# Attention scores on four 64x64 quarters of the array, in tiles of 64 queries by 192 keys

## The chip, the cores and the metric

The program runs on one core of one Trainium2 chip. The metric is the device time of one execution in microseconds (us). Names of engines: PE is the matrix engine (TensorE), PEld its weight loads, DVE the vector engine, ACT the scalar engine, POOL GpSimd, SP the engine that issues the DMAs. PSUM is the memory that PE writes, in banks.

## The reference, cut to what matters

Windowed attention (a query sees itself and the 127 keys before it, with a bias that falls linearly with distance, steeper for some heads), then a gated MLP whose gate mixes positions, then a token-shift block.

```python
def _attn_ref(q, k, v):                      # (4, 8, 576, 64) each
    scores = scale * q @ k.T
    rel = pos[:, None] - pos[None, :]
    slopes = 2.0 ** (-8.0 * (np.arange(H) + 1) / H)
    bias = slopes[:, None, None] * (-np.abs(rel))
    mask = (rel >= 0) & (rel < 128)
    scores = np.where(mask, scores + bias, -1e9)
    attn = exp(scores - max); attn = attn / (sum(attn) + 1e-09)
    return attn @ v
...
def _moe_ref(x, w_in, g_ln, w_sg, b_sg, w_out):   # x (4, 576, 512), d_ff 1024
    h = gelu(x @ w_in); u, v = h[..., :512], h[..., 512:]
    v_n = layernorm(v) * g_ln
    v_s = einsum('ts,bsd->btd', w_sg, v_n) + b_sg[None, :, None]
    return x + (u * v_s) @ w_out
...
def _moe2_ref(x, mu_k, mu_r, w_k, w_v, w_r):
    xk, xr = token-shift mixes of x
    return sigmoid(xr @ w_r) * (relu(xk @ w_k) ** 2 @ w_v)
```

## The kernel before

The 32 heads are taken in 16 pairs; a pair's q and k lie transposed in SBUF, one head on partitions 0 to 63 and the other on 64 to 127 (`rawqk`, 64 is the head's width). The MLP and the last block work in fp32r, the attention in full fp32: PE runs an fp32 matmul as two records in the trace, each streaming its columns twice.

**Scores.** `s_items` takes 128 queries by 256 keys (128 for the first tile): the two heads of a pair run side by side on the two halves of the array's rows, each into a PSUM bank of its own. The last 64 queries are one matmul of 64 by 192 for each head on two 64x64 quarters, into one bank (`last_items`). `s_tile` follows each score tile: DVE adds the mask and takes the row's extreme (`nmax`), ACT takes the exponential with the row sum, and, for heads from 8 on (`fold`), DVE or POOL adds the two key halves onto each other, so that 256 keys become 128 columns with two triangles to be told apart later.

**Probabilities times v.** The probabilities are turned by PE transposes (`t1_step`, `t2_step`, `t4_step`): 7 of them for each of the first 8 heads, 4 for a folded one, and 1 for a pair's last queries. For folded heads `keep` splits the triangles, on POOL by affine_select or on DVE by a multiplication with `tri`. `av_items` multiplies v (128 keys by 64) by up to 256 columns; the heads of a pair use the two halves of the array's columns.

**Where it stands.** `slot(c)` is the work of a pair. From pair 5 on two groups stand on PE: `av_s` (the pair before times v, then the first half of this pair's scores) and `s_rest` (the last 64 queries, then the second half). `moe1(b)` is the MLP of batch b; `merge` mixes the next pairs' attention into it. `phase2` is the last block. The mask comes from the DMA `rel`, the identity for transposes from the DMA `ident`; DVE and POOL turn `rel` into 8 masks and 4 for the last queries (`mask_head`).

**What sets the order.** A list scheduler in the kernel (`Rec.schedule`) orders the instructions of all engines by latest start plus the numbers in `PRI`, and picks the engine where there are several (`ENG`). Each engine then runs its queue strictly in that order. Where PE would stand empty early on, the scheduler puts filler matmuls (`wps<-tri`) that compute nothing.

Of the kernel before, what the change touches and what calls it, by code (L numbers as in the profile page):

```python
# [20 lines left out]
P = 128  # L21
# [27 lines left out]
    ("vsg", "dve/pool"): -122084, ("vsg.1", "dve"): 2660, ("vsg.1", "dve/pool"): -32242, ("w_in_t.0", "act/dve/pool"): -34846,
    ("w_in_t.0", "dve/pool"): 16462, ("w_out_t.1", "act/dve/pool"): 9, ("w_out_t.1", "dve/pool"): -16447, ("w_r_t", "act/dve/pool"): -4065,  # L50
    ("w_r_t", "dve/pool"): -22022, ("w_sg_t.1", "dve/pool"): -208885, ("w_v_t", "act/dve/pool"): -3901, ("w_v_t", "dve/pool"): -2737,
    ("wdec", "act"): 24174, ("wdec", "dve"): 74457, ("wdec.0", "dve"): 34851, ("wdec.1", "act"): 46, ("wdec.1", "dve"): 112585,
# [1284 lines left out]
```

## Time and profile before

| | us |
|---|---|
| device time, median of 3 runs (592.68 to 592.96) | 592.87 |
| span of the profiled execution, first to last instruction | 591.1 |
| PE busy | 578.8 (98%) |
| DVE, ACT, POOL busy | 422.5, 301.9, 158.4 |
| start to the first matmul with `w_sg` (0 to 92.81): PE, DVE busy | 85.96, 81.50 |
| 92.81 to 278.00 (attention inside the MLP): PE busy | 185.19 |
| 278.00 to 586.64 (rest of the MLP, last block): PE busy | 307.65 |

The profiled execution's own device time is not listed; its span stands 1.8 us under the median, which is what lies around the span. A busy PE includes fillers and weight loads that are not hidden, so a group's cost is read from the starts of the matmuls ahead of it and behind it, not from its busy time.

### The profile page before, as it was taken

The page shows a single profiled execution, that of the slowest core. Times are in us where ns is not written, and L with a number is a line of the kernel's source. Part 1 is how long each engine was busy: PE and PEld are TensorE (multiplying, and loading weights), DVE is VectorE, ACT ScalarE, POOL GpSimd, SP SyncE. Part 2 cuts the span into 40 slices and gives each one's busy share as a digit, 9 for nine tenths or more (in the row PEclk, how much of TensorE's full clock was granted, in tenths as well). Part 3 has the DMA queues.
Part 4 walks back from the last instruction along what each step waited for, and adds up shares of the span by engine and source line. Part 5 has one row for each costly group of instructions (what it writes and reads, how often), then busy time and mean ns, then how long its engine had stood idle before and what let it go on. Part 6 is the DMA issues. An engine that isn't in the chain of part 4 may idle for free.

```text
span 591.1 us, 10011 instructions
## 1 busy us (share of the span) xinstructions
PE 578.8 (98%) x3579; PEld 482.2 (82%) x3579; DVE 422.5 (71%) x1149; ACT 301.9 (51%) x790; POOL 158.4 (27%) x287
## 2 busy tenths in 40 slices
PE   7999999999999999999999999999999999999996
PEld 4666688987899878989799987888888888888895
DVE  5998999986979769887799999972945162615221
ACT  4977876646666546733564387440413441442141
...
DMA packets 23282, 48.29 MB, mean 82 GB/s; under 512 B 4416, under 2 KB 13120, under 8 KB 22720
## 3 DMA queue, kind: packets, MB, share of 16 engines
...
q14 instruction: 22, 0.18, 0.1%
...
## 4 chain that ended last, share of the span: by engine, by line
PE 87%; DMA 5%; DVE 4%; ACT 2%; issue 0%; POOL 0%; SPq 0%; ACTq 0%; DVEq 0%
PE d L466 51%; PE vps L466 17%; PE rps L466 8%; PE s L466 5%; PE a L466 4%; DMA st<-in_w_in_dram 3%; PE tf L474 2%; DMA rawv<-in_v_dram 1%; DMA rawqk<-in_qk_dram 1%; DVE p L810 1%; PE t L474 1%; ACT p L571 1%; DMA wraw<-in_w_sgT_dram 0%; DVE w_sg_t L508 0%; DVE wdec L561 0%
## 5 line engine op out<-in xcount | busy, mean ns | idle before, releaser
L466 PE MATMUL d<-xk,wk 128*128 128x512 f32 (+1 forms) x480 | 102.1, 368 | 0.0
L466 PEld LDWEIGHTS d<-xk,wk 128*128 128x128 f32 x480 | 84.0, 188 | 15.6
L466 PE MATMUL vps<-w_v_t,k2h 128*128 128x512 f32 x288 | 95.5, 395 | 0.0
L488 ACT ACTIVATE p<-p,nmax 128x256 f32<-128x256 f32 (+1 forms) x144 | 67.5, 471 | 29.1 <-DVE nmax L810 28.2
L466 PEld LDWEIGHTS vps<-w_v_t,k2h 128*128 128x128 f32 x288 | 54.1, 188 | 12.9
L466 PE MATMUL d<-w_sg_t,vhl 128*128 128x288 f32 x448 | 63.8, 298 | 0.0
L508 DVE TENSOR_TENSOR k2l<-rl,k2h 128x512 fp32r<-128x512 f32 (+1 forms) x40 | 24.9, 635 | 53.6 <-ACT k2h L496 53.1
L466 PEld LDWEIGHTS d<-w_sg_t,vhl 128*128 128x128 f32 x448 | 60.3, 188 | 2.0 <-issue 2.0
L466 PE MATMUL d<-w_in_t,xg 128*128 128x512 f32 (+1 forms) x240 | 60.9, 401 | 0.9 <-ACT xg L496 0.6
L466 PE MATMUL vps<-w_v_t,k2l 128*128 128x512 f32 x144 | 57.0, 396 | 0.0
L810 DVE CUSTOM_DVE_ANT_0 p<-s,mask 128x256 f32<-128x256 f32 (+1 forms) x144 | 48.1, 381 | 11.0 <-PE s L466 10.7
L466 PE MATMUL d<-gg,w_out_t 128*128 128x288 f32 x384 | 55.2, 297 | 0.0
L466 PE MATMUL rps<-w_r_t,xr 128*128 128x512 f32 x216 | 53.7, 392 | 1.0 <-ACT r L488 1.0
L466 PE MATMUL d<-xg,w_in_t 128*128 128x288 f32 x384 | 54.3, 298 | 0.2 <-DVE u L544 0.2
L466 PEld LDWEIGHTS d<-xg,w_in_t 128*128 128x128 f32 x384 | 51.6, 188 | 2.7 <-issue 1.0
L466 PEld LDWEIGHTS d<-gg,w_out_t 128*128 128x128 f32 x384 | 52.0, 188 | 1.8 <-issue 1.3
L466 PEld LDWEIGHTS d<-w_in_t,xg 128*128 128x128 f32 (+1 forms) x240 | 41.2, 177 | 15.0 <-issue 2.0
L466 PEld LDWEIGHTS rps<-w_r_t,xr 128*128 128x128 f32 x216 | 40.4, 188 | 10.4 <-ACT r L488 1.4
L508 DVE TENSOR_TENSOR r<-vps,r 128x512 f32<-128x512 f32 x18 | 12.4, 690 | 47.8 <-ACT r L488 32.9
L466 PE MATMUL s<-rawqk 64*128 64x256 f32 (+2 forms) x320 | 42.2, 371 | 1.8 <-DMA rawqk<-in_qk_dram 0.9
L488 ACT ACTIVATE rl<-d 128x512 f32<-128x512 f32 (+1 forms) x40 | 22.0, 554 | 41.9 <-PE d L466 36.4
L527 POOL TENSOR_SCALAR_AFFINE_SELECT pf<-pf 128x512 f32<-128x512 f32 (+2 forms) x58 | 34.0, 598 | 23.2 <-ACT pf L496 11.8
(120 smaller groups left out, 946.5 us busy)
## 6 DMA issues: line engine op xcount, KB each, us to landing
...
```

The costliest lines, as they stand in the source:

```text
L466: pe.matmul(real(o), real(l), real(r), start=st, stop=sp, **ex)
L474: pe.transpose(real(o), real(i), real(d))
L488: nc.scalar.activation(real(out), real(in_), func, scale=scale, **kw)
L508: alts.append(("dve", self._dve(out.n, False), lambda: nc.vector.tensor_tensor(real(out), real(a), real(b), op)))
L527: nc.gpsimd.affine_select(out=real(out), in_=real(in_), pattern=[[0, rows], [sgn, n]], compare_op=cmp, fill=0.0, base=0, channel_multiplie ...
L571: alts.append(("act", self._act(a, 1), lambda: nc.scalar.mul(real(out), real(a), real(s1))))
L810: K.raw("dve", 70 + w / 0.96, lambda: nc.vector.tensor_tensor_reduce(out=real(pw), in0=real(s), in1=real(ma), scale=-0.125, scalar=3.0e38, ...
```

## The change

Scores are taken in tiles of 64 queries, n = 0 to 8, by the 192 keys that they can see (64 and 128 for the first two). Query block n of head j goes to output partitions 64p with p = j for even n and the other half for odd n, so that four matmuls, two heads by two blocks, use the four 64x64 quarters; an even block and the odd one after it lie in two banks. The two heads of a pair share one tile of 128 partitions, with 9 tiles for a pair as before. Every tile with 192 keys is folded to 128 columns (7 for a pair, in all pairs), so all pairs need 9 transposes. In the products with v a matmul has 128 columns, not up to 256, and there are 14 where there were 8 (beside the 4 of 64 columns). `rel` and `ident` are made on POOL (iota, affine_select, memset), the DMAs for them go, and there are 4 masks of 2 by 192. `PRI` and `ENG` are new numbers throughout.

```diff
 PRI = {
...
-    rel = T("up", [P, MW], F32, "u", "rel")
+    rel = T("up", [P, 192], F32, "u", "rel")
-    K.tri = T("attc", [P, 2, 4, P], BF16, "tri")
+    K.tri = T("attc", [P, 2, 8, 64], BF16, "tri")
...
+    def s_item(c, n, bank, k):
+        w, k0 = width(n), 64 * max(n - 2, 0)
+        raw, it = rawqk[c], []
+        for p in range(2):
+            j = p ^ (n % 2)
+            r = slice(64 * j, 64 * j + 64)
+            it.append((bank[64 * p:64 * p + 64, k, 0:w], raw[r, 0, 64 * n:64 * n + 64], raw[r, 1, k0:k0 + w], True, True, SG))
+        return it
+    def s_items(c, half):
         banks = [T("psS", [P, 2, 256], F32, "s") for _ in range(2)]
-        for k, i in enumerate(ii):
-            q0 = i * P
-            k0, w = (q0 - P, 256) if i else (0, P)
-            for j in range(2):
-                r = slice(64 * j, 64 * j + 64)
-                it.append((banks[j][:, k, :w], rawqk[c][r, 0, q0:q0 + P], rawqk[c][r, 1, k0:k0 + w], True, True, {}))
+        return banks, [x for k in range(2) for o in range(2) for x in s_item(c, 4 * half + 2 * k + o, banks[o], k)]
...
-        if i == 4 or i and fold(n):
-            K.tt(p[:, :w - P], p[:, :w - P], p[:, P:w], ALU.add, "dp")
+        f = 64 if n % 2 and n > 1 else 0
+        if n > 1:
+            K.tt(p[:, 2 * f:2 * f + 64], p[:, 0:64], p[:, 128:192], ALU.add, "dp")
+        elif n == 0:
+            z = p[:, 64:128]
+            K.raw("pool", 110, lambda: nc.gpsimd.memset(real(z), 0.0), [], [z])
+        PT[c, n] = p[:, f:f + 128]
...
+    def t_step(c, b):
+        K.transposes([(t[:, 2 * i:2 * i + 2, :].flat(), PT.pop((c, 4 * b + i)), ident) for i in range(4)])
+        K.copy(pf[:, i0:i0 + 8, :].flat(), t.flat())
+        m = 4 if b == 0 else 0
+        K.keep(pf[:, 14 + i0 + m:22 + i0, :], pf[:, i0 + m:i0 + 8, :], True, "dp")
+        K.keep(pf[:, i0:i0 + 8, :], pf[:, i0:i0 + 8, :], False, "dp")
...
+        for t in range(4):
+            for j in range(2):
+                its.append((a[64 * j:64 * j + 64, 2 * t:2 * t + 2, :], rv[j][:, t, :], pair(4 * t, j), t == 0, t == 3, SG))
+            if t < 3:
+                for j in range(2):
+                    its.append((a[64 * j:64 * j + 64, 2 * t + 2:2 * t + 4, :], rv[j][:, t, :], pair(18 + 4 * t, j), False, False, SG))
...
-    K.dma(rel, relc, P * MW * 4)
-    K.dma(ident, identc, P * P * 4)
+    def rel_rows(v):
+        K.raw("pool", 290, lambda: nc.gpsimd.iota(...), [], [v])
+        K.raw("pool", 285, lambda: sel([[-1, 192]], 128, 1, ALU.is_ge), [v], [v])
+        K.raw("pool", 285, lambda: sel([[1, 192]], 0, -1, ALU.is_gt), [v], [v])
+    for j in range(2):
+        rel_rows(rel[64 * j:64 * j + 64])
...
+    def mask_pair(c):
+        K.ts(mask[:, c], mask[:, 0], 4.0 ** -c, 0.0, ALU.mult, ALU.add, "dp")
```

On PE, one pair inside the MLP. Names: `a` is the product with v, `s` a score bank, `tf` a transpose, `d` the MLP. Before, a pair inside a product with `w_out_t`:

```order
L466 MATMUL a<-pf,rawv 64x256 x6
L466 MATMUL a<-pf,rawv 64x128 x2
L466 MATMUL a_2882<-pf_2831,rawv 64x64 x4
L466 MATMUL s<-rawqk 128x128 x2
L466 MATMUL s<-rawqk 128x256 x2
L466 MATMUL d<-gg,w_out_t 128x288 x12
L466 MATMUL s<-rawqk 64x192 x2
L466 MATMUL s<-rawqk 128x256 x4
L466 MATMUL d<-gg,w_out_t 128x288 x42
```

and after, a pair inside a product with `w_out_t`:

```order
L472 MATMUL a<-pf,rawv 64x128 x14
L472 MATMUL a_1950<-pf,rawv 64x64 x4
L472 MATMUL s<-rawqk 64x64 x2
L472 MATMUL s<-rawqk 64x128 x2
L472 MATMUL s<-rawqk 64x192 x4
L472 MATMUL d<-gg,w_out_t 128x288 x18
L472 MATMUL s<-rawqk 64x192 x10
L472 MATMUL d<-gg,w_out_t 128x288 x42
```

The second score group had two forms, a 64x64 and a 64x128 one, and now has one form.

POOL at the start, before (`tri` is the triangle mask, `w_in_t` the split of the first weights):

```order
L1187 MEMSET tri 128x1024
L881 MEMSET x 128x4 x2
L527 ISA
L527 AFFINE_SELECT tri<-tri 128x512 x2
L564 TENSOR_SCALAR mask_147<-rel 64x192 x6
L564 TENSOR_SCALAR mask<-rel 128x320 x3
L510 TENSOR_TENSOR w_in_t<-wdec,w_in_t 128x512
```

and after:

```order
L1196 MEMSET ident 128x128
L820 MEMSET p 128x64 x2
L1197 ISA
L1197 AFFINE_SELECT ident<-ident 128x128
L820 MEMSET p 128x64
L1186 IOTA rel 64x192 x2
L1185 AFFINE_SELECT rel<-rel 64x192 x4
L877 MEMSET x 128x4
L1199 MEMSET tri 128x1024
L877 MEMSET x 128x4
L534 AFFINE_SELECT tri<-tri 128x512 x2
L516 TENSOR_TENSOR p<-p 128x64 x3
```

`tri` comes behind `rel` and `ident`; PE's filler ahead of the first score matmul reads `tri`. The eight subtractions that write `w_in_t`, all on POOL before, are on DVE after.

DVE's queue up to the first layernorm statistic of batch 0 (`bn`) changes by these counts. New: 8 subtractions `w_in_t` of 128x512, 20 folds `p` of 128x64, 6 triangle products `pf` of 128x128 and 2 of 128x256, 3 casts `xg` of 128x576, 2 products `p` with `rin`. Gone: 3 copies `pf` of 128x384 and 3 of 128x512 (one more of 128x512 comes from `tf`), 1 copy `rt`, 4 folds of 128x128, 1 cast `w_in_t`, 1 step `gt`. The score steps were 30 of 256 columns, 10 of 128 and 5 of 192, and are 35 of 192, 5 of 128 and 5 of 64; the masks were 5 of 320 and 2 of 64x192, and are 3 of 384 and 4 of 64x192.

PE at the program's end, before (`vps` and `rps` are the two products of the last block; `r` needs the sigmoid of `rps` and then `vps`):

```order
L466 MATMUL vps<-w_v_t,k2h 128x512 x2
L466 MATMUL vps<-w_v_t,k2l 128x512
L466 MATMUL vps<-w_v_t,k2h 128x512
L466 MATMUL rps<-w_r_t,xr 128x512 x12
L1333 UNCONDITIONAL_BRANCH
```

and after:

```order
L472 MATMUL rps<-w_r_t,xr 128x512 x12
L472 MATMUL vps<-w_v_t,k2h 128x512
L472 MATMUL vps<-w_v_t,k2l 128x512
L472 MATMUL vps<-w_v_t,k2h 128x512 x2
L472 MATMUL vps<-w_v_t,k2l 128x512
L472 MATMUL vps<-w_v_t,k2h 128x512 x2
L472 MATMUL vps<-w_v_t,k2l 128x512
L472 MATMUL vps<-w_v_t,k2h 128x512 x2
L472 MATMUL vps<-w_v_t,k2l 128x512
L472 MATMUL vps<-w_v_t,k2h 128x512
```

The last matmuls are now those of `vps`, not those of `rps`.

## Rows read from the trace of the kernel before

**Rows 1.** Stage; its length; busy PE, PEld, DVE, ACT, POOL; clock; DMA share, GB/s

```profile
0.00:92.81 92.81, 85.96 (x655) 61.91 (x656) 81.50 (x269) 70.01 (x221) 54.28 (x101) 1.00 0.61 171
92.81:278.00 185.19, 185.19 (x1409) 160.93 (x1408) 155.41 (x484) 106.10 (x328) 69.91 (x137) 1.00 0.18 53
278.00:586.64 308.64, 307.65 (x1519) 259.38 (x1518) 184.85 (x396) 125.24 (x241) 34.18 (x50) 1.00 0.22 71
```

**Rows 2.** The same view, stretches of ten us in the first fifty

```profile
10.00:20.00 10.00, 9.77 (x91) 6.67 (x88) 9.97 (x37) 9.36 (x34) 4.50 (x8) 1.00 1.03 318
...
40.00:50.00 10.00, 10.00 (x92) 7.24 (x90) 9.55 (x34) 7.63 (x28) 4.93 (x10) 1.00 0.49 124
```

**Rows 3.** PE in order of time, a second score group: start, us, form, records

```profile
217.29 0.86 PE L466 MATMUL d<-w_in_t,xg 128*128 128x512 f32 x3
217.76 0.40 PE L466 MATMUL d<-w_in_t,xg 128*128 128x512 f32 x1
218.09 0.38 PE L466 MATMUL s<-rawqk 64*64 64x192 f32 x2
218.30 0.75 PE L466 MATMUL s<-rawqk 64*64 64x192 f32 x4
218.56 0.70 PE L466 MATMUL s<-rawqk 64*128 64x256 f32 x4
218.88 0.81 PE L466 MATMUL s<-rawqk 64*128 64x256 f32 x6
219.31 0.38 PE L466 MATMUL s<-rawqk 64*128 64x256 f32 x2
219.62 0.50 PE L466 MATMUL d<-w_in_t,xg 128*128 128x512 f32 x1
```

**Rows 4.** The same view, a first score group and the MLP matmul behind it

```profile
214.24 0.93 PE L466 MATMUL s<-rawqk 64*128 64x128 f32 x8
215.09 0.50 PE L466 MATMUL d<-w_in_t,xg 128*128 128x512 f32 x1
```

**Rows 5.** Groups on PE from 100 to 278: records, busy us, mean ns

```profile
L474 PE MATMUL tf<-ident,p 128*128 128x128 f32 x81 | 11.9, 272 | 0.0
```

**Rows 6.** The end, ACT and DVE in order of time

```profile
586.68 0.60 ACT L488 ACTIVATE r<-rps 128x512 f32<-128x512 f32 x1 [0.76 <-PE rps L466]
587.31 0.69 DVE L508 TENSOR_TENSOR r<-vps,r 128x512 f32<-128x512 f32 x1 [0.67 <-ACT r L488]
```

**Rows 7.** Groups on DVE from 10 to 50, and on POOL from 0 to 59

```profile
L561 DVE TENSOR_SCALAR wdec<-wdec 128x512 uint32<-128x512 uint32 x8 | 7.7, 964 | 0.0
L810 DVE CUSTOM_DVE_ANT_0 p<-s,mask 128x256 f32<-128x256 f32 x28 | 10.3, 415 | 0.2
L810 DVE CUSTOM_DVE_ANT_0 p<-s,mask 128x192 f32<-128x192 f32 x4 | 1.4, 346 | 0.0
L498 DVE COPY pf<-t 128x512 f32<-128x512 f32 x3 | 2.1, 686 | 0.0
L510 POOL TENSOR_TENSOR w_in_t<-wdec,w_in_t 128x512 fp32r<-128x512 f32 x8 | 10.3, 1291 | 9.9 <-ACT w_in_t L496 4.8 <-DVE w_in_t L498 2.8 <-PE t L474 2.2
```

**Rows 8.** Groups on DVE, whole run

```profile
L508 DVE TENSOR_TENSOR w_v_t<-wdec,w_v_t 128x512 fp32r<-128x512 f32 x8 | 5.5, 689 | 1.2 <-ACT w_v_t L496 1.1
L508 DVE TENSOR_TENSOR p<-p 128x64 f32<-128x64 f32 x8 | 1.8, 219 | 0.4 <-ACT p L488 0.4
```

**Rows 9.** DVE, PE and POOL in order of time, early

```profile
16.04 0.36 DVE L561 TENSOR_SCALAR wdec<-wdec 128x512 uint32<-128x512 uint32 x1
6.05 0.92 PE L466 MATMUL s<-rawqk 64*128 64x128 f32 x6 [0.74 <-DMA rawqk<-in_qk_dram]
8.01 0.27 DVE L810 CUSTOM_DVE_ANT_0 p<-s,mask 128x128 f32<-128x128 f32 x1
1.85 1.23 POOL L527 TENSOR_SCALAR_AFFINE_SELECT tri<-tri 128x512 bf16<-128x512 bf16 x2
58.69 0.68 DVE L1003 BATCH_NORM_STATS2 bn<-v 128x6 f32<-128x512 f32 x1
```

More of the change, by code (lines that the diff above doesn't have):

```diff
@@ L49 @@
[L49 to L52, printed above, removed]
[6 rows of a table removed]
[3 rows of a table added]
@@ L102 @@
 MERGE = 5
-FOLD = 8
 PLAIN_S = ()
@@ L530, in keep @@
         if "p" in engs and not in_.ps:
-            alts.append(("pool", 137 + 0.715 * out.n + 10 * (rows - 1), go))
-        m = self.tri[:, int(upper), :rows, :n]
+            alts.append(("pool", 147 + 0.715 * out.n, go))
+        t = self.tri[:, int(upper), :m, :]
         if "d" in engs:
-            alts.append(("dve", self._dve(out.n, False), lambda: nc.vector.tensor_tensor(real(out), real(in_), real(m), ALU.mult)))
-        return self.r.op(alts, [in_] + ([m] if "d" in engs else []), [out])
+            alts.append(("dve", self._dve(out.n, False), lambda: nc.vector.tensor_tensor(real(out), real(in_), real(t), ALU.mult)))
+        return self.r.op(alts, [in_] + ([t] if "d" in engs else []), [out])
     def sub(self, out, a, hi, engs="dp"):
@@ L774, in r_rows, with s_bank @@
         return rt
-    def s_bank(c, ii):
-        banks, it = s_items(c, ii)
+    def s_bank(c, half):
+        banks, it = s_items(c, half)
         K.mm(it)
-        s_tiles(c, ii, banks)
+        s_tiles(c, half, banks)
     def s_last(c):
@@ L799, in av_s, with s_tile @@
         a, a4b, it = av_items(c - 1, "psT")
-        banks, its = s_items(c, (0, 1))
+        banks, its = s_items(c, 0)
         AV.append(K.mm(it + its))
         av_copy(c - 1, a, a4b)
-        s_tiles(c, (0, 1), banks)
-    def s_tile(c, n, i, s, ma, col):
-        p = T("sp", [P, 256], F32, "p")
+        s_tiles(c, 0, banks)
+    def s_tile(c, n, bank):
+        p = T("sp", [P, 192], F32, "p")
         na = T("st", [P, 1], F32, "nmax", bufs=8)
-        w = s.n
-        po = pw = p[:, :w]
+        w = width(n)
+        s, po, ma = bank[:, :w], p[:, :w], mask[:, c % (H // 2), n % 2, 192 - w:192]
@@ L834, in t2_step @@
-    def t2_step(n):
-        if fold(n):
-            return
-        t = T("psT", [P, 4, P], F32, "t")
-        K.transposes([(t[:, j, :], PT[n, i][:, c:c + P], ident) for j, (i, c) in enumerate(((2, P), (3, 0), (3, P)))])
-        K.copy(PTc[n][:, 4:7, :], t[:, 0:3, :])
-        for i in range(4):
-            PT.pop((n, i))
+        K.act(po, po, ACTF.Exp, bias=na, scale=-1.0, accum=SUM[c][:, n:n + 1])
+        f = 64 if n % 2 and n > 1 else 0
[4 more added lines that the diff above has]
+            K.raw("pool", 110, lambda: nc.gpsimd.memset(real(z), 0.0), [], [z])
@@ L866, in av_items @@
[L866 to L868 removed]
+        a = T("psD", [P, 8, 64], F32, "d", "a") if c >= NC else T("psT", [P, 8, 64], F32, "t", "a")
+        a4b = T(pool, [P, 2, 256], F32, "s" if pool == "psS" else "t", "a4")[:, 0, 0:64]
+        pf, its = PTc.pop(c), []
@@ new lines, in av_items, with pair @@
+        rv = [rawv.pop(2 * c + j) for j in range(2)]
+        def pair(i, j):
+            lo, hi = i + j, i + 3 - j
+            return pf[:, min(lo, hi):max(lo, hi) + 1:abs(hi - lo), :]
+        for t in range(4):
[4 more added lines that the diff above has]
+                    its.append((a[64 * j:64 * j + 64, 2 * t + 2:2 * t + 4, :], rv[j][:, t, :], pair(18 + 4 * t, j), False, False, SG))
@@ L870, in av_step @@
+        for k, i in ((3, 30), (4, 16)):
+            for j in range(2):
+                its.append((a4b[64 * j:64 * j + 64], rv[j][:, k, :], pf[:, i + j, :], k == 3, k == 4, SG))
+        return a, a4b, its
     def av_step(c):
@@ L918, in trans @@
         def trans():
-            for j in range(2):
-                add(480, t1_step, 2 * prev + j)
-                add(340, t2_step, 2 * prev + j)
+            for b in range(2):
+                add(480, t_step, prev, b)
             add(120, t4_step, prev)
@@ L934, in slot @@
         if cur:
-            add(1000, s_bank, c, (0, 1))
+            add(1000, s_bank, c, 0)
         if has:
@@ L938, in slot @@
         if cur:
-            add(1000, s_bank, c, (2, 3))
+            add(1000, s_bank, c, 1)
         if has:
@@ L1183, in attn_gmlp_rwkv_kernel, with sel @@
     K.mm([(wps, wz[:, 0:128], wz, True, True, {})] * NWARM)
-    warm = (K.tri[:, 0, 0, :], K.tri[:, 0].flat()[:, 0:256], 220)
+    warm = (K.tri[:, 0].flat()[:, 0:128], K.tri[:, 0].flat()[:, 0:256], 220)
     load_pair(0)
-    K.dma(rel, relc, P * MW * 4)
-    K.raw("pool", 1100, lambda: nc.gpsimd.memset(real(K.tri), 1.0), [], [K.tri])
+    def rel_rows(v):
+        def sel(pat, base, mult, cmp):
+            nc.gpsimd.affine_select(out=real(v), in_=real(v), pattern=pat, compare_op=cmp, fill=FAR, base=base, channel_multiplier=mult)
+        K.raw("pool", 290, lambda: nc.gpsimd.iota(
+            real(v), pattern=[[-1, 192]], base=128, channel_multiplier=1, allow_small_or_imprecise_dtypes=True), [], [v])
+        K.raw("pool", 285, lambda: sel([[-1, 192]], 128, 1, ALU.is_ge), [v], [v])
+        K.raw("pool", 285, lambda: sel([[1, 192]], 0, -1, ALU.is_gt), [v], [v])
+    for j in range(2):
+        rel_rows(rel[64 * j:64 * j + 64])
+    for j in range(2):
+        r = slice(64 * j, 64 * j + 64)
+        for o in range(2):
+            K.ts(mask[r, 0, o, :], rel[r], -8.0 * 2.0 ** -((j ^ o) + 1), 0.0, ALU.mult, ALU.add, "d")
+    K.raw("pool", 250, lambda: nc.gpsimd.memset(real(ident), 1.0), [], [ident])
+    K.raw("pool", 240, lambda: nc.gpsimd.affine_select(
+        out=real(ident), in_=real(ident), pattern=[[1, P]], compare_op=ALU.is_equal, fill=0.0, base=0, channel_multiplier=-1), [ident], [ident])
+    K.raw("pool", 950, lambda: nc.gpsimd.memset(real(K.tri), 1.0), [], [K.tri])
     for u in range(2):
         K.keep(K.tri[:, u], K.tri[:, u], bool(u))
-    K.dma(ident, identc, P * P * 4)
     load_v(0)
@@ L1193, in attn_gmlp_rwkv_kernel @@
     load_pair(1)
-    def mask_head(h):
-        slope = -8.0 * 2.0 ** -(h + 1)
-        K.ts(mask[:, h, :], rel, slope, 0.0, ALU.mult, ALU.add, "dp")
-        j = h % 2
-        r = slice(64 * j, 64 * j + 64)
-        K.ts(mask4[r, h // 2, :], rel[r, 64 + 64 * j:256 + 64 * j], slope, 0.0, ALU.mult, ALU.add, "dp")
-    for h in range(2):
-        mask_head(h)
+    def mask_pair(c):
+        K.ts(mask[:, c], mask[:, 0], 4.0 ** -c, 0.0, ALU.mult, ALU.add, "dp")
     K.dma(gln2, g_ln.rearrange("(c p) -> p c", p=P), 2048)
```

202 lines of the change are left out of this document (89 added, 113 removed), and 43 rows, old and new, of the table PRI.

## The prediction

> **What bounds the kernel now.** First the busy times by stage [rows 1]. From 92.81, the first matmul with `w_sg`, to 278.00 PE is busy for all of 185.19 us, and from there to 586.64 for 307.65 of 308.64, at the full clock (1.00, its upper level of 2.4 GHz). So behind 92.81 only less work on PE, or a shorter end, can shorten the run; DVE is busy for 155.41 of 185.19 there and can wait. Before 92.81 it is otherwise: PE's 85.96 contain fillers, and in the stretches of ten us DVE is busy for 9.97 and 9.55 [rows 2]. That stage goes at DVE's pace, with PE close behind (9.77 and 10.00). The sum therefore has three parts: PE's work in the attention behind 92.81, the stage ahead of it, and the end.
>
> **Part 1, the score groups behind 92.81.** The transposes on PE between 100 and 278 are 81, nine for a pair [rows 5], so nine pairs lie here (pairs 7 to 15). Read a second score group from start to start [rows 3]. The MLP matmuls ahead start 0.235 apart (two steps from 217.29 to 217.76); from the last of them the first score record follows after 0.33 (218.09), so entering the group costs 0.10. An fp32 record passes its columns twice: 192 columns are 0.16, 256 are 0.21. The first record takes 0.21 (218.09 to 218.30), 0.05 over its stream; the second 0.26 (to 218.56), 0.10 over it, which is the change of form from 64x64 to 64x128; the first of the new form 0.32 (to 218.88), 0.11 over it. I read the 0.05 and 0.11 as the first weights of 64 and 128 columns, which nothing hides. Then 0.43 for two, on schedule, the last 0.31 (219.31 to 219.62), 0.10 over, and the MLP matmul behind takes 0.50, not 0.40. The group costs 0.10 + 1.53 + 0.10 = 1.73 us, of which 1.17 are streams (2 x 0.16 + 4 x 0.21).
>
> After the change this group is 10 matmuls of 192 columns in one form. With four quarters at once the two of the last queries and the eight others make three rounds of two records: 6 x 0.16 = 0.96. Entering costs 0.10 + 0.05, leaving 0.10 + 0.10; the inner change of form is gone. That is 1.31, or **0.42 less**. The first score group runs from 214.24 to 215.09, 0.85 [rows 4]: streams 2 x 0.107 + 2 x 0.213 = 0.64 (128 and 256 columns), the rest first weights and leaving. After, the longer pair of quarters streams 128 + 192 columns twice each, 0.53, with 0.05 and 0.10 around it: 0.68, or **0.16 less**. The product with v streams as many columns as before in more matmuls; the added starts I put at 0.01, bounded by 0 and by 0.1 (a tenth of what it costs to leave a form, were each seam to show). So a pair costs 0.57 less, nine pairs **5.1 us**. Bounds: 4.3 if each product with v costs 0.1 more, 5.3 if it costs nothing and an even block runs ahead.
>
> That four run at once no row shows. The rows show two on the rows' halves in two banks, and two quarters of one bank (the two records of 218.09 together last 0.38, as long as one) [rows 3]; the four combine these.
>
> **Part 2, the stage ahead of 92.81.** PE gets less work here too: seven pairs at about 0.57, and in each of the first four pairs 9 transposes instead of 15, 24 fewer at 0.11 (128 columns twice), together 6.6 us, less 0.7 for the five pairs whose groups stand apart and share no change of form: 5.9. But DVE sets the pace, so I count its queue up to the first layernorm statistic, at 58.69 [rows 9]. More: 8 subtractions at 0.69 and 20 folds at 0.22 [rows 8], 8 triangle products at an estimated 0.35 (a score step of 192 columns is 0.346 [rows 7]), 3 casts and 2 products at 0.4 (the shift alone is 0.36 [rows 9]): 14.7. Less: 7 copies out of PSUM of 384 or 512 columns (0.686 for 512 [rows 7]), of which one comes back, 3.7; score steps, 0.415 at 256 columns and 0.346 at 192 [rows 7], so on their line 0.28 at 128 and 0.21 at 64: 17.0 (30, 5 and 10 of them) become 14.6 (35 of 192, 5 and 5), 2.4 less; 4 folds, a cast, a step and the difference in masks, about 2.9. That is 5.7 us more; records on DVE overlap by some 0.05 and there are about 25 more of them, which leaves **4.5 more**.
>
> Against it stands what POOL no longer does. The shifts of `wdec` take 0.964 on average between 10 and 50 [rows 7] and 0.36 where nothing disturbs them [rows 9]: eight of them lose 4.8 us, while POOL's eight subtractions `w_in_t` run, 1.291 each [rows 7]. These go to DVE, so the loss goes: **4.8 less**. The Trainium skill, "SBUF — State Buffer", section SBUF: two separate sides, says of the port pair that VectorE and GpSimd share: whichever starts first gets the pair for its whole instruction and the other is fully blocked. Were DVE to lose each of the eight subtractions whole by that rule, 10.3 us would come back and the sum would be 580.0; the shifts show 4.8 of it [rows 7].
>
> The start: DVE's first score step stands at 8.01, though the score group starts at 6.05 and takes 0.92 [rows 9]: DVE was still making masks from `rel`. After, `rel` and `ident` are made on POOL ahead of `tri`, and PE's filler that reads `tri` stands in PE's queue ahead of all scores. So this adds a wait: everything on PE behind that filler. No row shows an iota. POOL's two selects of 512 columns take 1.23 [rows 9]; a tile of 64x192 at a third to a whole of one of them (0.2 to 0.6), six of them 1.3 to 3.7, and `ident` with the zeros 0.5 to 1.0, put the end of `tri`, now 3.08, at 4.9 to 7.8. The first scores would start at 6.05 to 8.1, the first step at 7.1 to 9.1, 0.9 earlier to 1.1 later. The tile is three eighths of a select's columns, so I take the low side, 0.6 earlier. The masks that DVE made after its first steps are made ahead of them, 0.4. Up to 92.81 DVE's queue then loses another 0.4 in score steps. Sum: + 4.5 - 4.8 - 0.6 - 0.4 - 0.4 = **1.7 us earlier**. ACT and POOL have less or as much to do here, the two DMAs gone are 224 KB of a queue that moved 318 GB/s [rows 2], 0.7 us that I count at nothing since DVE covers it. PE follows, 5.9 us of its work less, so it isn't the bound.
>
> **Part 3, the end.** Before, ACT's sigmoid starts at 586.68 and DVE's product behind it at 587.31 [rows 6]; after, the last matmuls are `vps`, whose sigmoid is done, and the 0.63 goes. **0.6 less.** The wait of 1.0 in the last stage (308.64 against 307.65 [rows 1]) I leave where it is.
>
> **Sum.** 5.1 + 1.7 + 0.6 = 7.4. It is made against the span, 591.1 to 583.7; with the 1.8 around it that is 592.9 - 7.4 = **585.5 us**.
>
> **Rivals.** *Quarters go two at a time (slower).* Each round of four becomes two: 0.53 more in a first group, 0.64 in a second, 1.17 a pair. Nine pairs then cost 9 x (1.17 - 0.57) = 5.4 more; ahead of 92.81 seven pairs add 8.2 to PE's 5.9 less, so PE is late by up to 2.3, take 1; with the end, 5.4 + 1.0 - 0.6 = 5.8 more: **598.7**. It decides from about 0.8 us a pair lost, two rounds in three. In its favour: four at once isn't in the trace, and the seams cost what they cost with two. Against: both kinds of pair run fully side by side, and a row half doesn't hold up the other [rows 3]. The Trainium skill, "TensorEngine Tiling (Array Packing)", Gotcha 1 under Restrictions and Gotchas, says that different row tiles cannot access the same PSUM bank simultaneously; by it the two quarters that share a bank here would take turns, the 598.7. The records of 218.09, which share a bank on two halves of the rows, speak against that here. Chance 0.1.
>
> *The early stage takes DVE's added work and gets nothing back.* POOL's many folds (3 in a row ahead of its first select) hold up DVE as its subtractions did, or the start is late: up to + 4.5 where I have - 1.7: 5.1 + 0.6 - 4.5 = 1.2 less, **591.7**; half of it, 588.6. Chance 0.15.
>
> *PE sets the early stage after all.* It was at 10.00 of 10 from 40 to 50 [rows 2]. Then its 5.9 count: 5.1 + 5.9 + 0.6 = 11.6 less, **581.3**. Chance 0.13.
>
> **How the numbers follow.** My forecast, 582.5 to 588.5 around 585.5, has 0.6; the rest, 0.02, is a new wait that I don't see. The range 580.5 to 590.5 takes in the third rival and most of the second. Within 0.2% means 591.7 to 594.1, about what a measurement here can tell from no change. Faster: 0.6 + 0.13 + most of 0.15, 0.84; same 0.04; slower 0.12.
>
> **What would show it.** Right: in the last stage a second score group of about 1.2 us from its first record to the MLP matmul behind it, four quarter records starting within some 0.03 us, PE still without gaps behind the first `w_sg` matmul, and that matmul 1 to 3 us earlier than 92.81; `wdec` near 0.36. Wrong: quarter records in pairs 0.3 apart; a first score step behind 8.0; DVE's shifts still near 1 us; PE waiting for DVE or POOL behind 92.81.

## The result, and the profile after

The changed kernel took 587.78 us (median of four runs, 585.60 to 587.97) against 592.91 for the kernel before beside it: ratio 0.9899, 95% interval 0.9886 to 0.9912, 5.1 us less. The forecast was 585.5 with a range of 580.5 to 590.5. The profiled execution took 587.97, its span is 586.3.

One correction first. The prediction calls 92.81 [rows 1] the first matmul with `w_sg`. That boundary lies five records late; by its own row in PE's order of time (start, us, form, records) it stands at 92.14, and all comparisons below start there:

```profile
92.14 3.10 PE L466 MATMUL d<-w_sg_t,vhl 128*128 128x288 f32 x22
```

The changed kernel by stages (stage; its length; busy PE, PEld, DVE, ACT, POOL; clock; DMA share, GB/s), as [rows 1]. Its first `w_sg` matmul starts at 93.79:

```profile
0.00:93.79 93.79, 84.62 (x857) 62.21 (x858) 83.64 (x302) 67.24 (x219) 49.06 (x104) 0.95 0.61 165
93.79:278.00 184.21, 184.21 (x1700) 167.63 (x1699) 143.42 (x457) 108.38 (x338) 93.03 (x170) 1.00 0.21 60
278.00:586.26 308.26, 304.17 (x1496) 256.20 (x1494) 187.96 (x416) 114.11 (x222) 34.84 (x48) 1.00 0.21 70
```

Behind the first `w_sg` matmul all went as forecast, and a little better: 591.1 - 92.14 = 499.0 us became 586.3 - 93.79 = 492.5, 6.5 less (forecast 5.7). Ahead of it the run became 1.65 longer, where 1.7 less were forecast. The 0.95 in the clock column is new: before, it was 1.00 throughout. (This column counts nothing ahead of the first clock record; see the section on the start.)

**The score groups.** PE in order of time, a second score group in the changed kernel, as [rows 3], and a product with v with a first score group, as [rows 4]:

```profile
214.13 0.86 PE L472 MATMUL d<-w_in_t,xg 128*128 128x512 f32 x3
214.92 1.19 PE L472 MATMUL s<-rawqk 64*64 64x192 f32 x20
216.04 0.73 PE L472 MATMUL d<-w_in_t,xg 128*128 128x512 f32 x2
...
230.37 1.98 PE L472 MATMUL a<-pf,rawv 128*64 128x128 f32 x36
232.28 0.77 PE L472 MATMUL s<-rawqk 64*64 64x64 f32 x16
232.99 1.19 PE L472 MATMUL d<-xg,w_in_t 128*128 128x288 f32 x7
```

The 20 records of the second group last 214.92 to 216.04, 1.12. Read from start to start as the prediction does (0.09 to enter, 0.10 to leave), the group costs 1.31; over the nine pairs it went from 15.6 to 11.9 us, 0.41 each (forecast 0.42). Product and first group last 2.62 (230.37 to 232.99). Before, a product started here, and the MLP matmul behind its group at 215.09 [rows 4], 2.75 later:

```profile
212.34 1.97 PE L466 MATMUL a<-pf,rawv 128*64 128x256 f32 x24
```

Over nine pairs that is 0.14 less each (forecast 0.15).

**The clock.** Windows of the changed kernel (columns as above) around the two stretches with the lower of PE's two levels, 1.2 instead of 2.4 GHz, and PE's and DVE's order of time there (in brackets the idle time before, and who ended it):

```profile
21.00:22.00 1.00, 0.16 (x2) 0.00 (x0) 1.00 (x3) 0.57 (x1) 0.00 (x0) 1.00 0.76 214
22.00:23.00 1.00, 0.18 (x4) 0.19 (x4) 1.00 (x3) 1.00 (x4) 0.00 (x0) 1.00 0.78 225
...
24.00:28.00 4.00, 4.00 (x30) 2.66 (x34) 3.82 (x14) 3.35 (x12) 3.04 (x5) 0.50 0.96 232
28.00:32.00 4.00, 4.00 (x53) 2.76 (x47) 2.13 (x13) 3.75 (x14) 1.17 (x4) 0.76 1.03 270
54.00:57.00 3.00, 1.45 (x7) 0.41 (x7) 2.97 (x10) 0.76 (x4) 0.00 (x0) 1.00 0.36 106
57.00:60.00 3.00, 2.75 (x8) 2.16 (x9) 2.77 (x10) 1.76 (x5) 0.84 (x2) 0.54 0.97 254
```

```profile
22.82 0.33 PE L472 MATMUL s<-rawqk 64*64 64x64 f32 x4 [1.66 <-ACT x L502]
23.87 1.33 PE L472 MATMUL s<-rawqk 64*64 64x128 f32 x12 [0.72 <-DVE nmax L811]
...
56.45 0.50 PE L472 MATMUL d<-w_in_t,xg 128*128 128x512 f32 x1 [1.46 <-DVE xg L504]
...
29.05 0.36 DVE L811 CUSTOM_DVE_ANT_0 p<-s,mask 128x192 f32<-128x192 f32 x1 [1.23 <-PE s L472]
```

In the kernel before the same stretch read so:

```profile
20.00:24.00 4.00, 3.02 (x30) 1.80 (x25) 4.00 (x10) 3.60 (x11) 1.90 (x2) 1.00 1.05 360
```

In the changed kernel PE stands nearly empty from 21.2 to 23.9; the granted clock is 0.50 from 23.1 to 30.0; and DVE, which was to set the pace of this stage, waits 1.23 us for scores. The same again at 55 to 61, shorter. Before, PE's longest empty stretch between 10 and 92 us was 0.77; here two of 1.66 and 1.46 stand there. Whether the work that is gone opened them or the new order of all instructions, no run separates.

**The start** (answers [rows 9]). The two `tri` selects end later than before, as named (6.53, not 3.08), and PE's filler waits for the first of them, its start being ahead of the second one's end; the first score step of DVE stands at 7.41:

```profile
5.18 1.35 POOL L534 TENSOR_SCALAR_AFFINE_SELECT tri<-tri 128x512 bf16<-128x512 bf16 x2
5.92 0.39 PE L472 MATMUL wps<-tri 128*128 128x256 bf16 x1 [1.05 <-POOL tri L534]
6.24 1.35 PE L472 MATMUL s<-rawqk 64*64 64x64 f32 x16
7.41 0.23 DVE L811 CUSTOM_DVE_ANT_0 p<-s,mask 128x64 f32<-128x64 f32 x1 [0.61 <-PE s L472]
```

**DVE's groups** from 10 to 50 (line, operation, shapes, records; busy us, mean ns; idle before), which answer [rows 7, 8]. The shift is no longer stalled; the folds cost 0.26, not 0.22, the subtractions 0.75, not 0.69:

```profile
L514 DVE TENSOR_TENSOR w_in_t<-wdec,w_in_t 128x512 fp32r<-128x512 f32 x7 | 5.2, 755 | 0.1
L514 DVE TENSOR_TENSOR p<-p 128x64 f32<-128x64 f32 x15 | 3.7, 259 | 0.0
L568 DVE TENSOR_SCALAR wdec<-wdec 128x512 uint32<-128x512 uint32 x8 | 3.3, 417 | 0.0
```

**The end** (answers [rows 6]). No sigmoid stands between the last matmul and DVE's product. The wait in the last stage that the prediction left alone shrank too; of the two rows below the first is of before, the second of after:

```profile
364.26 2.11 PE L466 MATMUL rps<-w_r_t,xr 128*128 128x512 f32 x8 [0.99 <-ACT r L488]
```

```profile
360.29 1.42 PE L472 MATMUL rps<-w_r_t,xr 128*128 128x512 f32 x5 [0.31 <-ACT r L494]
...
582.09 0.39 PE L472 MATMUL vps<-w_v_t,k2h 128*128 128x512 f32 x1
582.59 0.69 DVE L514 TENSOR_TENSOR r<-vps,r 128x512 f32<-128x512 f32 x1 [0.77 <-PE vps L472]
```

So 6.5 is 4.8 from the groups on PE (second groups 15.6 to 11.9; products with first groups, entering and leaving counted in, 26.5 to 25.3; less 0.1 for transposes that stand otherwise), 0.7 from that wait, 0.6 from the sigmoid and 0.15 from the last product to the end; 0.3 is left over.

### The profile page after: what moved, and what is told of

It is laid out like the page before. It is cut to its first block, busy times and chain, and to the rows that moved or that the text cites. A ratio compares the mean times of both kernels' runs of the same rounds, so it can differ in the third digit from the quotient of the medians.

```text
span 586.3 us, 11019 instructions
## 1 busy us (share of the span) xinstructions
PE 573.0 (98%) x4050; PEld 486.0 (83%) x4050; DVE 415.0 (71%) x1174; ACT 289.7 (49%) x778; POOL 176.9 (30%) x321
## 4 chain that ended last, share of the span: by engine, by line
PE 85%; DVE 10%; ACT 1%; issue 1%; POOL 1%; DMA 1%; SPq 0%; POOLq 0%; DVEq 0%; ACTq 0%
PE d L472 50%; PE vps L472 17%; PE rps L472 8%; PE s L472 4%; PE a L472 4%; PE tf L480 2%; DVE p L811 2%; DVE wdec L551 1%; DMA wraw<-in_w_sgT_dram 1%; DVE wdec L568 1%; DVE gt L551 1%; DVE p L514 0%; DVE v L551 0%; DVE w_sg_t L514 0%; DVE bn L998 0%
## 5 line engine op out<-in xcount | busy, mean ns | idle before, releaser
L472 PE MATMUL vps<-w_v_t,k2h 128*128 128x512 f32 x288 | 93.7, 396 | 0.0
L494 ACT ACTIVATE p<-p,nmax 128x192 f32<-128x192 f32 (+2 forms) x144 | 61.5, 429 | 30.0 <-DVE nmax L811 29.6
L472 PE MATMUL d<-w_in_t,xg 128*128 128x512 f32 (+1 forms) x240 | 63.1, 410 | 2.0 <-DVE xg L504 1.5
L472 PEld LDWEIGHTS vps<-w_v_t,k2h 128*128 128x128 f32 x288 | 54.1, 188 | 12.9
L534 POOL TENSOR_SCALAR_AFFINE_SELECT pf<-pf 128x512 f32<-128x512 f32 (+2 forms) x70 | 43.4, 636 | 37.2 <-ACT pf L502 20.7
L811 DVE CUSTOM_DVE_ANT_0 p<-s,mask 128x192 f32<-128x192 f32 (+1 forms) x144 | 41.2, 328 | 8.1 <-PE s L472 8.1
L506 POOL TENSOR_SCALAR xk<-mt 128x64 fp32r<-128x64 f32 (+4 forms) x9 | 6.9, 766 | 130.6 <-DVE mt L551 129.3
L494 ACT ACTIVATE r<-rps 128x512 f32<-128x512 f32 x18 | 10.7, 599 | 66.3 <-PE rps L472 66.2
```

The lines of the kernel that those rows point to most:

```text
L472: pe.matmul(real(o), real(l), real(r), start=st, stop=sp, **ex)
L494: nc.scalar.activation(real(out), real(in_), func, scale=scale, **kw)
L506: alts.append(("pool", 148 + 0.83 * in_.n, lambda: nc.gpsimd.tensor_scalar(real(out), real(in_), 1.0, 0.0, ALU.mult, ALU.add)))
L534: nc.gpsimd.affine_select(out=real(out), in_=real(in_), pattern=pat, compare_op=cmp, fill=0.0, base=0, channel_multiplier=-sgn)
L811: K.raw("dve", 70 + w / 0.96, lambda: nc.vector.tensor_tensor_reduce(out=real(po), in0=real(s), in1=real(ma), scale=-0.125, scalar=3.0e38, ...
```

## The experiments

What had to be explained was the stage ahead of `w_sg`: forecast 1.7 shorter, measured 1.65 longer. The theory: PE's clock, which the prediction had taken as 1.00 throughout, fell, and made PE late for DVE. The rival: DVE sets the pace, PE's clock costs nothing, and the sum for DVE was wrong. The table has all medians, and from the one profiled run of each kernel the first `w_sg` matmul and the stretches at the lower level (what stands ahead of the first clock record is not listed). The profiled run is not always near the median: it took 587.97 (changed kernel), 587.19 (after_again), 584.24 (fill_first and no_fill) and 584.69 (wf_pe_early).

| kernel | device time, median (range) | ratio to before, 95% | first `w_sg` | clock at 0.50 |
|---|---|---|---|---|
| changed kernel | 587.78 (585.60-587.97) | 0.9899 [0.9886, 0.9912] | 93.79 | 23.1-30.0, 57.3-60.7 |
| the same again (after_again) | 585.75 (585.46-588.05) | 0.9879 [0.9861, 0.9896] | 92.71 | 8.4-11.8, 22.1-28.9, 56.2-59.6 |
| fill_first | 585.19 (584.24-585.92) | 0.9859 [0.9842, 0.9877] | 90.09 | 53.2-56.7 |
| fill_second | 583.67 (583.63-586.85) | 0.9856 [0.9830, 0.9881] | 89.48 | 7.6-11.0 |
| fill_both | 584.65 (583.70-584.86) | 0.9848 [0.9832, 0.9864] | 90.43 | none recorded |
| no_fill | 586.78 (584.24-587.43) | 0.9891 [0.9871, 0.9910] | 89.94 | 12.1-15.5, 22.4-25.8 |
| warm10 | 584.22 (584.19-584.32) | 0.9844 [0.9831, 0.9858] | 89.95 | 22.6-26.0 |
| warm_fill | 583.51 (583.32-583.91) | 0.9832 [0.9819, 0.9846] | 89.12 | none |
| wf_two_quarters | 604.10 (603.29-604.66) | 1.0176 [1.0162, 1.0190] | 99.13 | 79.1-85.9 |
| wf_subs_on_pool | 583.83 (583.59-584.30) | 0.9836 [0.9820, 0.9853] | 89.66 | none |
| wf_pe_early | 583.66 (583.49-584.69) | 0.9838 [0.9824, 0.9851] | 89.80 | none recorded |
| wf_pe_late | 583.95 (583.91-584.07) | 0.9840 [0.9827, 0.9853] | 89.73 | none |
| wf_dve_early | 585.71 (585.25-585.87) | 0.9868 [0.9855, 0.9882] | 91.70 | 49.8-53.2 |

### Fillers where PE stood empty

Extra fillers are put into PE's finished queue, all else in its place:

```diff
     order = R.schedule()
+    def pad(name, k, w, n):
+        at = [i for i, o in enumerate(order) if o.pe and o.lab == name][k]
...
+        order[at:at] = many
+    pad("s.0", 6, 0, 13)
+    pad("d.1", 0, 1, 12)
```

The first call alone is fill_first, the second alone fill_second, both are fill_both; no_fill drops the planned fillers instead:

```diff
     order = R.schedule()
+    order = [o for o in order if o.lab != "fill"]
```

> The changed kernel with 13 more filler matmuls (wps from tri, 128x256 bf16, about 0.12 us each) on PE ahead of the first score group of pair 3, where PE stood empty from 21.2 to 22.8 and the granted clock then fell to 0.50 for 6.8 us. Theory A (the fall follows the empty stretch, and for as long as it lasts PE is what DVE waits for): the first fall is gone, the clock of the run is 0.997, and the time is that of the one run of the changed kernel that had this clock, 585.6 (585.2 to 586.2), the first w_sg matmul at about 92. Theory B (DVE paces this stage, PE's clock costs nothing in it): the clock may rise but the time stays at 587.8 (587.4 to 588.2). Theory C (the fall comes for another reason): the clock falls all the same, 587.8.

> The changed kernel with 12 more fillers on PE ahead of the first matmul of w_in_t with xg behind the second filler start, where PE stood empty from 55.0 to 56.5 and the clock then fell to 0.50 for 3.4 us. A: the second fall is gone, the run's clock is 0.994, and the time is 586.7 to 587.6: half of 3.4 us is 1.7, of which some hides behind DVE. B and C: 587.8, in C with the clock unchanged at 0.991.

> Both sets of fillers. A: clock 1.000, the two gains add, 584.4 to 585.6, and the first w_sg matmul stands at 91 to 92, near the 91.1 that the sum for this stage gave. B: 587.8 with a clock of 1.000. C: 587.8 with a clock of 0.991.

> The changed kernel with the 30 planned fillers left out and every other instruction in its place. A: the clock falls more often or for longer between 12 and 60 us, a run's clock of 0.95 to 0.985, and the stage ahead of the first w_sg matmul grows by 3 to 10 us: 590 to 598. B: the clock falls as under A and the time stays within 1 us of 587.8. C: neither moves.

fill_both against the changed kernel's profile is the clean pair, since both start alike (first score step at 7.40 and 7.41); these two runs took 584.63 and 587.97. Its windows, the counterparts of those above:

```profile
20.00:24.00 4.00, 3.05 (x34) 2.22 (x35) 4.00 (x11) 2.41 (x6) 0.72 (x2) 1.00 0.64 161
...
28.00:32.00 4.00, 3.94 (x59) 2.91 (x59) 3.73 (x17) 3.98 (x13) 1.06 (x4) 1.00 1.02 281
```

With PE kept busy the clock holds, DVE is busy for 3.73 of the 4 us in which it had 2.13, and the first `w_sg` matmul moves from 93.79 to 90.43: the two falls cost 3.4 us. fill_first took the first fall away as theory A says (585.19; three of its four runs have the clock of 0.997); its profiled run, the fastest, had an early first rise as well, so its 90.09 (A: about 92) is not the price of the first fall alone. But A is too simple, and two kernels show it. fill_second leaves the first hole open (now at 20.1 to 22.8), and its clock held over it:

```profile
20.00:24.00 4.00, 1.59 (x21) 1.09 (x21) 4.00 (x10) 2.90 (x7) 1.17 (x2) 1.00 0.93 211
```

Three of its five runs took 583.6, better than A allowed, two took 586.8, these with a mean clock of 0.994 and not 0.996. And no_fill, without any of the planned fillers, took 586.78, no worse than the changed kernel, where A expected 590 to 598; in its profiled run, its fastest (584.24), both falls are short. So falls stand behind empty stretches, but an empty stretch does not bring one each time; the planned fillers in other places did little. What decides it is not settled by these runs.

### The start

A second thing differs between the traces. The changed kernel and fill_both have their first full-clock record only at 12.9 and 12.6 us, the other four traces up to then (before among them) at 4.0 to 5.5. Until it, PE works at half speed: in the changed kernel fillers start 0.21 apart at 11 us and 0.11 apart in warm_fill, and the first score group takes 1.35 instead of 0.78. In the changed kernel PE stands empty ahead of this from 4.86 to 5.92, waiting for `tri`. Two more of the first matmuls cover all but 0.2 us of that while PE is still slow:

```diff
     order = R.schedule()
+    def rewarm(n):
+        at = next(i for i, o in enumerate(order) if o.lab == "wps")
...
+        order[at + 1:at + 1] = many
+    rewarm(2)
```

This alone is warm10; with both sets of fillers it is warm_fill. Beside warm_fill the changed kernel ran again.

> The changed kernel again, unaltered, for its spread on the same chip as the next three. Theory A (falls of the granted clock early on cost what the time varies by): runs with a mean clock of 0.991 have a span of 585.6 to 586.3, runs of 0.994 about 584 to 585.2, runs of 0.997 about 582.5 to 584; most runs 0.991. Rival (the clock is not the cause): spans vary without regard to the mean clock.

> Both sets of fillers, and two more of the first matmuls (wps from wz, 128x512) at the very start, which cover the stretch from 4.86 to 5.9 in which PE stood empty for want of tri. In two of the six traces so far the first full-clock entry stands only at 12.6 to 12.9 us and the first score group takes 1.35 us; in the other four it stands at 4.1 to 5.5 and the group takes 0.78. Theory R (the empty stretch is why the rise is missed): the rise stands at 4 to 6 in every run, the first score step of DVE at 6.8, the first w_sg matmul at 89.0 to 89.9, spans 581.3 to 582.3, 583.0 to 584.0. Rival (the rise is missed by chance): spans spread as with both fillers alone, 582.0 to 583.1, 583.7 to 584.9.

> The changed kernel with two more of the first matmuls at the start (PE no longer empty from 4.86 to 5.9) and no other fillers. Theory A + R (the start decides when the full clock begins, the empty stretches at 21 and 55 decide whether it falls later): the first full-clock entry at 4 to 6 us and the first score step at 6.8 in every run, but falls at about 22 and 55 remain; mean clock 0.991 to 0.997 and 583.5 to 586.5 with a spread of 1 us or more. Rival (the start alone decides, the falls later don't cost): all runs within 0.6 us of each other at 583.3 to 583.9.

The start of warm_fill:

```profile
5.91 0.28 PE L472 MATMUL wps<-tri 128*128 128x256 bf16 x1 [0.63 <-POOL tri L534]
6.12 0.77 PE L472 MATMUL s<-rawqk 64*64 64x64 f32 x16
6.83 0.22 DVE L811 CUSTOM_DVE_ANT_0 p<-s,mask 128x64 f32<-128x64 f32 x1
```

(PE is empty for 0.63 here, since its clock had risen at 4.70 and the two matmuls were over sooner.) The group takes 0.77, the first step comes at 6.83 instead of 7.41, the first `w_sg` matmul at 89.12, and five runs lie within 0.6 us: 583.51, as R expected, 1.7% under the kernel before and the fastest of all. The changed kernel beside it again ran at 585.46 to 588.05. Three of its five runs have a mean clock of 0.997, where most were expected at 0.991. Its spans follow its mean clock as expected (583.7 to 584.0 at 0.997, 586.3 at 0.991), with one exception: the profiled run has a mean of 0.988 and only 585.5. It has the two falls of the changed kernel and a third from 8.4 to 11.8; but its clock rose at 4.99, not 12.9, its first step stands at 6.83, and a late rise does not enter the mean. warm10 splits the two repairs. The expectation that its runs would spread by 1 us or more failed: all four took 584.2 to 584.3, each with one short fall by its mean clock of 0.997 (22.6 to 26.0 in the trace), and the fall at 55 did not come. That fall costs 0.7 us against warm_fill; so the two matmuls at the start alone bring the ratio from 0.9879 to 0.9844, as much as all 25 fillers do (0.9848). Theory R, that the empty stretch causes the late rise, is favoured but not proven: where the rise was early, it came ahead of that stretch or at its start (4.14 and 4.99 in fill_second and after_again), and in wf_pe_early, below, with the two matmuls and PE empty for only 0.20, it still came late in the profiled run, though at 7.29 and not at 12.6.

### Four quarters or two

```diff
     for p in range(2):
-        j = p ^ (n % 2)
+        j = p
         r = slice(64 * j, 64 * j + 64)
```

> The kernel warm_fill with the score matmuls of odd blocks on the same two quarters of the array as those of even blocks, (rows 0 to 63, columns 0 to 63) and (rows 64 to 127, columns 64 to 127), so that only two can run at once; in odd blocks the two heads' scores thereby change places. Streams are the same. Theory F (four quarters run at once, and that is the gain): a first group costs 0.53 and a second 0.64 more, 1.17 us a pair; 10.5 us for nine pairs behind the first w_sg matmul and 0 to 8 ahead of it, 594 to 600. Rival (the gain is in fewer seams and forms, quarters of one half of the columns take turns anyway): within 1 us of warm_fill.

PE in order of time, the group of the rows at 214.92 above:

```profile
225.32 0.86 PE L472 MATMUL d<-w_in_t,xg 128*128 128x512 f32 x3
226.11 1.84 PE L472 MATMUL s<-rawqk 64*64 64x192 f32 x20
227.88 1.43 PE L472 MATMUL d<-w_in_t,xg 128*128 128x512 f32 x5
```

The same 20 records take 1.77 instead of 1.12, 0.65 more (expected 0.64), and the first group 0.43 more (0.53). In all 20.6 us are lost against warm_fill, and the 604.10 lies beyond the 594 to 600 expected. By the spans of the profiled runs it is 21.1: 11.1 behind the first `w_sg` matmul (expected 10.5; the groups of nine pairs are 9.7 of it, a new wait of PE at 243.7 is 0.8) and 10.0 ahead of it (0 to 8), where a fall from 79.1 to 85.9 adds to it. So the four quarters do run at once, and the change lives by it: with two at a time it is slower than the kernel before.

### The subtractions back on POOL

```diff
+    for o in order:
+        if o.lab == "w_in_t.0" and [a[0] for a in o.alts] == ["dve", "pool"]:
+            o.eng = o.alts[1]
```

> The kernel warm_fill with the eight subtractions that write w_in_t on POOL, as in the kernel before, all else in its place. Theory S (POOL's subtractions hold up DVE's shifts): the shift of wdec takes 0.75 to 1.0 on average again, not 0.42; DVE gives away 8 x 0.75 = 6.0 us and gets back 8 x 0.4 = 3.2 to 8 x 0.55 = 4.4 of stalls, and folds and selects on POOL wait behind 1.29 us each: the first w_sg matmul 2 us earlier to 3 us later, 581.5 to 586.5. Rival (the stalls come from somewhere else): the shift stays at 0.42 and the first w_sg matmul comes 3 us or more earlier, unless PE or ACT takes over.

Groups on DVE up to 58 us, warm_fill first, then with the subtractions on POOL:

```profile
L514 DVE TENSOR_TENSOR w_in_t<-wdec,w_in_t 128x512 fp32r<-128x512 f32 x8 | 5.9, 748 | 0.1
L514 DVE TENSOR_TENSOR p<-p 128x64 f32<-128x64 f32 x22 | 5.9, 286 | 1.0 <-ACT p L494 1.0
L568 DVE TENSOR_SCALAR wdec<-wdec 128x512 uint32<-128x512 uint32 x8 | 3.3, 417 | 0.0
L514 DVE TENSOR_TENSOR xg<-x,xg 128x576 fp32r<-128x576 f32 x3 | 2.3, 782 | 0.1
L568 DVE TENSOR_SCALAR sum<-sum 128x9 f32<-128x9 f32 x5 | 1.6, 329 | 0.0
```

```profile
L514 DVE TENSOR_TENSOR p<-p 128x64 f32<-128x64 f32 x22 | 6.8, 331 | 1.2 <-ACT p L494 1.2
L568 DVE TENSOR_SCALAR wdec<-wdec 128x512 uint32<-128x512 uint32 x8 | 3.7, 478 | 0.0
L514 DVE TENSOR_TENSOR xg<-x,xg 128x576 fp32r<-128x576 f32 x3 | 3.2, 1080 | 0.1
L568 DVE TENSOR_SCALAR sum<-sum 128x9 f32<-128x9 f32 x5 | 2.8, 566 | 0.0
```

Both theories missed on the shift: it takes 0.48, not 0.75 to 1.0. The stalls came all the same, on other instructions of DVE beside a subtraction: a tiny addition on `sum` went from 0.33 to 0.57, a subtraction `xg` from 0.78 to 1.08. These four rows hold 3.6 us of the 6.0 that DVE gave away (with the products of `pf` by `tri` and of `p` by `rin` and the casts `xg` it is 5.1), and the first `w_sg` matmul came 0.5 later. Moving them is a trade without gain, as the prediction's 5.5 for eight subtractions and 4.8 for the stalls said. Which instruction is the victim the order of time shows; two subtractions of wf_subs_on_pool, each with an instruction of DVE beside it:

```profile
17.52 1.29 POOL L516 TENSOR_TENSOR w_in_t<-wdec,w_in_t 128x512 fp32r<-128x512 f32 x1
17.62 1.27 DVE L514 TENSOR_TENSOR p<-p 128x64 f32<-128x64 f32 x1
...
41.58 1.30 POOL L516 TENSOR_TENSOR w_in_t<-wdec,w_in_t 128x512 fp32r<-128x512 f32 x1 [0.42 <-ACT w_in_t L502]
42.15 0.35 DVE L811 CUSTOM_DVE_ANT_0 p<-s,mask 128x192 f32<-128x192 f32 x1
```

The fold, 0.29 on average in warm_fill, ends 0.08 behind the subtraction: it stood until POOL was done. The score step, which reads the bank `s` in PSUM, took its usual 0.35, and so did copies out of PSUM and the addition of `a` (0.68) beside a subtraction. All the stalled rows named here have every operand in SBUF. So what is lost is the rest of the subtraction from the moment that DVE's order comes to such an instruction.

### Who sets the pace of the early stage

```diff
     pad("d.1", 0, 1, 12)
+    pad("d.0", 6, 0, 10)
```

is wf_pe_early; wf_pe_late has `pad("d.1", 6, 1, 10)` instead; wf_dve_early adds to DVE at the first of these places:

```diff
+        at = [i for i, o in enumerate(order) if o.pe and o.lab == "d.0"][6]
...
+            o.i, o.lab, o.pe, o.eng = 0, "mhalf", False, ("dve", 0, lambda: nc.vector.memset(real(mhalf), -0.5))
...
+    busy_dve(20)
```

> The kernel warm_fill with 10 more fillers (1.15 us of PE) in the middle of the early stage, at about 43 us. If DVE sets the pace there, the first w_sg matmul stays within 0.3 of 89.1 and the time within 0.3 of 583.5; if PE does, 90.0 to 90.3 and 584.6.

> The kernel warm_fill with 10 more fillers (1.15 us of PE) at about 64 us, in the stretch from the first layernorm statistic to the first w_sg matmul, where PE is busy for 97 in 100 and DVE for 99. If PE sets the pace there (PE's smaller work then explains why this stretch became 3.0 us shorter, 34.12 to 31.13, and not 0.4): first w_sg matmul at 90.0 to 90.3, 584.6. If DVE does: 89.1, 583.5. Both in turn: in between.

> The kernel warm_fill with 20 memsets of a 128x1 tile added on DVE (59 ns each by the one that is there, 1.2 us), at the same place in the order, about 43 us. If DVE sets the pace there: first layernorm statistic at 59.0 to 59.2 instead of 57.99, first w_sg matmul 0.8 to 1.2 later than 89.1, 584.3 to 584.7. If PE does: within 0.3 of 583.5.

(The 34.12 in these lines has the boundary that the first section corrects; to 92.14 it is 33.45.) wf_pe_early: 583.66, so PE does not set the pace around 43 us. Three runs took 583.5 to 583.7; the other two 584.6 and 584.7, and the profiled one of these shows why: its first full-clock record stands at 7.29, its first score group takes 1.26, and its first step stands at 7.41 again. wf_dve_early in order of time:

```profile
44.70 2.33 DVE L1272 MEMSET mhalf<- 128x1 f32 x19
...
60.55 0.69 DVE L998 BATCH_NORM_STATS2 bn<-v 128x6 f32<-128x512 f32 x1
```

The 20 memsets took DVE 2.4 us, not 1.2, since they start 0.125 apart and last 0.06. The statistic went from 57.99 to 60.55, the first `w_sg` matmul from 89.12 to 91.70, the time to 585.71: most of what is put on DVE there arrives at the end: 2.2 us, and 1.9 by span in the one run of clock 1.000 (the profiled run has a fall from 49.8 to 53.2, which is part of its 2.6). wf_pe_late: 583.95, 0.4 more of 1.15 (warm_fill's own runs spread by 0.6); that fits PE and DVE setting the pace in turns there, as the expectation put it, but lies little beyond the spread.

## Why the prediction was right or wrong, point by point

**What bounds the kernel: right.** PE alone behind `w_sg`, DVE up to the first statistic (wf_dve_early and wf_pe_early, both built on warm_fill).

**Part 1, the score groups: right, by its own terms.** Second group 1.73 to 1.31 forecast, 1.31 measured; first group with the product 0.15 less forecast, 0.14 measured; nine pairs 5.1 forecast, 4.8 measured, the rest being transposes that were not in the sum. Rival 1 (two at a time) was built: the group lost 0.65 where 0.64 was priced; the whole came to 604.1, not 598.7, since its first `w_sg` matmul stood 7.0 later than before (99.13, one fall ahead of it), where the price had 1. The rule that the prediction set beside it (the Trainium skill, "TensorEngine Tiling (Array Packing)", Gotcha 1 under Restrictions and Gotchas: different row tiles cannot access one PSUM bank at the same time) does not hold here: each bank is written by two row halves at once, and the group takes 1.12, not the 1.77 of taking turns.

**Part 2, the early stage: wrong in the sign, by 3.4 us.** The term that failed is one that the sum did not have: it took PE's clock as 1.00 because [rows 1] showed it so, and did not ask whether holes would open in PE's queue after which it may fall. The falls cost 3.4 (fill_both), a late rise at the start another 1.3 (89.12 against 90.43). Without them the stage is not 1.7 but 3.0 shorter (92.14 to 89.12). The pieces:
- The start: 0.6 earlier forecast, 0.6 measured (7.41), but with PE at half speed; at the full clock it is 1.2 (6.83). `tri` ended at 6.53, in the forecast's 4.9 to 7.8, but PE's filler needed only its first half and started at 5.92.
- DVE's queue to the statistic: 58.69 became 57.99 in warm_fill, 0.7 less where 1.3 was forecast, although the start gave 0.6 more. Without the start the sum was 1.2 too low. DVE's busy time up to the statistic rose by 2.8 (49.87 to 52.66), where + 4.5 - 4.8 had it fall by 0.3. Of that the 20 added folds are 1.5 (0.286 each, not 0.22), the lesser items 1.1 (the masks took more, not less), the subtractions 0.5 (0.748, not 0.69), the shifts 0.5 (0.417, not 0.36) and the triangle products 0.5. What made up for most of it is DVE's idle time there, 8.8 before and 5.3 now, which the sum had counted only at the start.
- The relief of the shifts: right in size as a trade (5.1 against 4.8), wrong in kind: the shift has only 0.5 of it (wf_subs_on_pool). The rule on the shared port (the Trainium skill, "SBUF — State Buffer", section SBUF: two separate sides: whichever starts first holds the pair for its whole instruction) agrees with the fold of 17.62, which stood until the subtraction was done. But DVE lost some 0.6 us for each subtraction, not its whole 1.29, since it went on with instructions that read PSUM until it came to one that was held, and the 580.0 did not come.
- The statistic to `w_sg`: 0.4 less forecast, 2.3 measured (33.45 to 31.13). Here rival 3 was half right. The rows of that stretch:

```profile
58.69:92.14 33.45, 32.72 (x236) 25.60 (x236) 30.99 (x104) 26.39 (x84) 21.52 (x43) 1.00 0.35 101
```

```profile
57.99:89.12 31.13, 30.23 (x283) 24.97 (x284) 30.93 (x108) 25.35 (x83) 22.08 (x43) 1.00 0.38 101
```

PE was busy for 98 in 100 of it before and has 2.5 us less to do; DVE has as much as before. The prediction read PE's fullness from 40 to 50 and dismissed it; where it counted was behind 58. That PE's smaller work is the cause there is read from these rows; wf_pe_late supports it in part.

**Part 3, the end: right**, 0.6. The wait that was left alone gave 0.7 more.

**Sum.** Span 583.7 forecast, 586.3 measured. That is 581.6 for the undisturbed kernel (2.1 better than forecast: 1.3 ahead of `w_sg`, 0.8 behind), plus 1.3 for the late rise, plus 3.4 for the falls. The forecast was near because two errors cancel in part, which is luck. Of the signs that it named, the group of 1.12, four quarter records within 0.03 us (214.92 to 214.95) and PE without gaps behind `w_sg` showed; the first `w_sg` matmul 1 to 3 us earlier did not, and the shift took 0.42.
